# A wait on VectorE for each GpSimd power, with the instruction orders left as they are

## The chip, the cores and the metric

One kernel runs on one core of a Trainium2 chip. The metric is the device time of one execution in microseconds (us). The core's engines run their own instruction streams and meet only at semaphores: TensorE (PE in the profile, with its weight loads as PEld), VectorE (DVE), ScalarE (ACT), GpSimd (POOL) and SyncE (SP), which here only issues transfers.

## What is computed

The reference is one transformer block over 2048 positions and 640 channels, in bfloat16. Cut to what matters:

```
x  = A_q
kv = shift(A_k, 4 taps) * A_v
y  = causal_conv(kv, ssm_k) + kv * ssm_D          # by FFT in the reference
h  = x + layernorm(x) * y
h2 = h + (silu(ln(h) @ w_gate) * (ln(h) @ w_up)) @ w_down
```

There are two layer norms, `layernorm(x)` and `ln(h)`. Each needs, for every position, the mean and one over the square root of the variance plus a small constant.

## The kernel before

**Tiling.** The 2048 positions are cut into four blocks of 512, called j = 0 to 3 in names. A block is 128 partitions by 4 rows (index b); the 640 channels are two halves of 320 (index c). The convolution of block 0 is done with dense transform matrices, that of later blocks with two transform steps on TensorE (`s1`, `s2`), complex products on VectorE (`m1`, `m2` multiply; `ac` adds; `cr`, `ci` combine) and an inverse (`i2`, `i1`). The feed-forward part of a block has, for each slice f of 128 inner channels, two matmul groups (`gu`), a silu on ScalarE (`si`), a copy of the second group out of PSUM by ScalarE into one small buffer (`ue`), and a multiplication on VectorE that reads this buffer (`gm`). There is only one such buffer (pool `UE`), so `ue` of a slice waits for `gm` of the slice before. The `kv` product of blocks 2 and 3 (`kvm`, `kvv`) adds its taps by accumulating transfers that GpSimd issues (`kvd`, line 1089). All matmuls of the main kind show up as line 694, all VectorE tensor-by-tensor operations as line 913, ScalarE's copies out of PSUM as line 677; a name such as `m1003` is product `m1` of block 0, half 0, part 3.

**The norm's statistics.** Each of the two norms ends, for a group of rows, in `ln_rstd` (lines 1009 to 1022), three tiny operations on 128x4 or 128x2 numbers: `va` on VectorE (line 1018, variance plus constant), `nr` on GpSimd (line 1019, power to -0.5) and `nm` on VectorE (line 1021, minus mean times the result). A normalization (`q`, `hn`, lines 1028 and 1029) reads the results of `nr` and of `nm`, on VectorE or ScalarE. `nr` exists 12 times: `nr0j` once per block (the four 128x4), `nr1j` twice per block (the eight 128x2).

**What sets the order.** The program first collects all operations with their dependences, and a planner (`Prog.schedule`) then plays them through with assumed durations and fixes the order on each engine. Priorities and some choices of engine come from a written list (`_ORDER`, `_WHO`). `emit` then writes, for each engine in that order, the semaphore waits that follow from each operation's `deps`, and the operation. A wait stands in front of its operation in the engine's own stream, so what is behind it on that engine is held too.

**The shared port in the planner.** VectorE operations whose names begin with `m1`, `m2`, `ac`, `kv`, `cr`, `ci`, `hn`, `nm`, `q`, `h`, `o` (the last three followed by a digit) or, for blocks 0 and 1, `gm`, carry `o.lock`: the planner takes them to use a port that VectorE shares with GpSimd. It lets no power begin while such an operation runs, and begins no such operation while a power runs (`poolend`). These two rules only shape the planned order. In the program that is written, nothing keeps the two apart.

The planner assumes 0.75 us for a power.

Of the kernel before, what the change touches and what calls it, by code (L numbers as in the profile page):

```python
# [106 lines left out]
class Prog:  # L107
# [147 lines left out]
    def schedule(self, bias):  # L255
        self.dnow, self.rings, self.waiting = 0.0, {"sp": [], "pool": [], "act": []}, []
        self.clock = {"k": -1, "s": 0.5, "busy": {}}
        pemode, dvelock, poolend = 0, False, 0.0
        free = {e: 0.0 for e in self.ENG}
        order = {e: [] for e in self.ENG}  # L260
        ready = []
        for o in self.ops:
            o.ready = o.minready
            if o.npred == 0:
                ready.append(o)
        t = 0.0
        left = len(self.ops)
        while left:
            done_any = True
            while done_any:  # L270
                done_any = False
                for e in ("pe", "dve", "act", "sp", "pool"):
                    if free[e] > t + 1e-9:
                        continue
                    best, held = None, set()
                    waits = e == "dve" and free["pool"] <= t + 1e-9 and any(
                        p.dma is None and p.engs.get("pool", 0) > 0.5 and p.ready <= t - 0.6 for p in ready if "pool" in p.engs)
                    for o in sorted((o for o in ready if e in o.engs and o.force in (None, e) and o.ready <= t + 1e-9), key=lambda o: (o.prio, o.idx)):
                        c = o.engs[e]
                        if e == "pool" and o.dma is None and c > 0.5 and free["dve"] > t + 1e-9 and dvelock:  # L280
                            continue
                        if e == "dve" and o.lock and (poolend > t + 1e-9 or waits):
                            continue
                        if e == "dve" and "act" in o.engs and not o.force:
                            if max(t, free["act"]) + o.engs["act"] <= t + c + bias:
                                continue
                        if e == "act" and "dve" in o.engs and not o.force:
                            if max(t, free["dve"]) + o.engs["dve"] + bias < t + c:
                                continue
                        ok = True  # L290
                        want = {}
                        for tl in o.tiles:
                            if tl.live:
                                continue
                            pl = self.pools[tl.pool]
                            n = want.get(tl.pool, 0)
                            if pl.inorder and (pl.at + n >= len(pl.seq) or pl.seq[pl.at + n] is not tl):
                                ok = False
                                break
                            if tl.pool in held:  # L300
                                ok = False
                                break
                            want[tl.pool] = n + 1
                        if not ok:
                            continue
                        for pn, n in want.items():
                            if sum(1 for f in self.pools[pn].free if f[0] <= t + 1e-9) < n:
                                ok = False
                                if n > 1:
                                    held.add(pn)  # L310
                        if ok:
                            best = o
                            break
                    if best is None:
                        continue
                    o = best
                    done_any = True
                    ready.remove(o)
                    left -= 1
                    for tl in o.tiles:  # L320
                        if not tl.live:
                            pl = self.pools[tl.pool]
                            pl.free.sort(key=lambda f: f[0])
                            _, tl.base, tl.prev = pl.free.pop(0)
                            tl.live = True
                            if pl.inorder:
                                pl.at += 1
                    o.eng, o.start = e, t
                    o.pos = len(order[e])
                    order[e].append(o)  # L330
                    for tl in o.tiles:
                        tl.touch.append(o)
                    if e == "dve":
                        dvelock = o.lock
                    if e == "pool" and o.dma is None and o.engs[e] > 0.5:
                        poolend = t + o.engs[e]
                    if o.dma is None:
                        c = o.engs[e] - self.OVERLAP[e]
                        if e == "pe":
                            c += 0.105 if o.mode != pemode else 0.0  # L340
                            pemode = o.mode
                        free[e] = self.pe_end(t, c, o.slow) if e == "pe" else t + c
                        self.release(o, free[e])
                    else:
                        free[e] = t + o.engs[e]
                        w, pkt, _ = o.dma
                        self.rings[e].append([o, w, pkt, free[e] + self.LEAD])
                    ready += self.waiting
                    self.waiting = []
            nxt = [f for f in free.values() if f > t + 1e-9] + [o.ready for o in ready if o.ready > t + 1e-9]  # L350
            for pl in self.pools.values():
                nxt += [f[0] for f in pl.free if f[0] > t + 1e-9]
            nxt += self.dma_next()
            if not nxt:
                if left:
                    raise RuntimeError("stuck: " + "; ".join(
                        f"{o.name}[{','.join(x.name for x in o.tiles if not x.live)}]" for o in ready[:20]))
                break
            t = max(t, min(nxt))
            self.drain(t)  # L360
            ready += self.waiting
            self.waiting = []
        self.drain(1e6)
        self.order = order
        self.span = max(o.finish for o in self.ops)
# [1024 lines left out]
```

## Time and profile before

| what | value |
|---|---|
| median of four runs | 297.8 us |
| the four runs | 297.42, 298.03, 300.35, 297.56 us |
| the profiled execution: its own time | 297.42 us |
| its span in the profile | 295.6 us |
| so, around the span | 1.8 us |
| TensorE busy | 280.0 us, 95% of the span |
| VectorE busy | 235.5 us, 80% |
| ScalarE busy | 200.5 us, 68% |
| GpSimd busy | 33.2 us, 11% |
| granted TensorE clock | 1.00 of full in every stretch |

Engines are named as above. A row of a timeline has the start in us from the span's beginning, the length in us from the first start to the last end, the engine, the line, the operation with its output and input, how many instructions are merged in the row, and in brackets the idle time before it and who ended it. Rows of VectorE can overlap a little, since one operation starts while the last one drains. A row of waits has who waited for whom, the total in us, how often, and the longest. TensorE's busy time is that of pipelined matmuls with modelled ends, so a busy TensorE is not one at its peak.

### The profile page before, as it was taken

The numbers are of one execution on the slowest core, as the hardware profiler recorded it, in microseconds if no ns is written. First come the engines' busy times: TensorE is split into PE (matmuls) and PEld (weight loads), VectorE is DVE, ScalarE is ACT, GpSimd is POOL, SyncE is SP. The second block draws the span as 40 slices with busy tenths as digits, with TensorE's granted clock in tenths as the row PEclk, the third lists the DMA queues.
The fourth block names the chain that finished last, engine by engine and source line by source line (L and its number), as shares of the span: only waits on it lengthen the run. The fifth ranks groups of instructions, "written<-read, shape, count | busy, mean of one in ns | idle before, by whom it ended". The sixth has DMA issues, their size and how long they took to land.

```text
span 295.6 us, 5187 instructions
## 1 busy us (share of the span) xinstructions
PE 280.0 (95%) x1801; PEld 153.1 (52%) x1820; DVE 235.5 (80%) x479; ACT 200.5 (68%) x484; POOL 33.2 (11%) x31
## 2 busy tenths in 40 slices
PE   7889979799999799999999999999999999999996
PEld 2456645454444366664445467654444676444574
DVE  3999899998999889999999999992899743214422
ACT  3389889999988878778899895768995221242000
POOL 2000500208111130101100304000020020000000
PEclk9999999999999999999999999999999999999999
DMA  6999999834685787727812038754001142000001
GB/s 190 318 354 376 290 365 329 282 116 128 169 179 151 178 205 202 222 73 196 222 41 96 9 83 211 169 137 179 19 0 44 47 90 75 16 0 0 2 22 67
DMA packets 44051, 43.25 MB, mean 146 GB/s; under 512 B 14895, under 2 KB 38889, under 8 KB 43898
## 3 DMA queue, kind: packets, MB, share of 16 engines
q1 hardware_dynamic: 39640, 38.30, 41.6%
q0 software_dynamic: 3328, 3.97, 8.3%
q10 hardware_dynamic: 1058, 0.66, 0.8%
q8 instruction: 14, 0.23, 0.4%
q14 instruction: 11, 0.09, 0.1%
HBM read 20.63 MB, written 2.62 MB: 79 GB/s over the span
## 4 chain that ended last, share of the span: by engine, by line
PE 68%; DVE 12%; ACT 8%; DMA 5%; POOL 3%; issue 2%; SPq 0%; ACTq 0%; DVEq 0%
PE ps L694 67%; DVE sb L913 10%; ACT sb L677 6%; DMA sb<-sb 5%; POOL stt L1019 3%; ACT sb L1029 1%; ACT sb L680 1%; PE ps L823 1%; DVE sb L678 0%; DVE sb L1028 0%; PE ps L1223 0%; DVE sb L681 0%; DVE sb L779 0%; ACT sb L1049 0%; ACT sb L1249 0%
## 5 line engine op out<-in xcount | busy, mean ns | idle before, releaser
L694 PE MATMUL ps<-sb 128*128 128x320 bf16 (+1 forms) x1201 | 224.2, 339 | 8.2 <-DVE sb L913 1.9
L913 DVE TENSOR_TENSOR sb<-sb 128x1280 bf16<-128x1280 bf16 (+3 forms) x286 | 171.0, 656 | 4.0 <-ACT sb L677 3.5
L694 PEld LDWEIGHTS ps<-sb 128*128 128x128 bf16 (+1 forms) x1220 | 116.1, 98 | 100.6 <-issue 8.2
L677 ACT ACTIVATE sb<-ps 128x320 bf16<-128x320 f32 (+2 forms) x282 | 111.5, 483 | 26.0 <-PE ps L694 21.2
L694 PE MATMUL ps<-sb,tab 128*64 128x320 bf16 (+2 forms) x512 | 63.3, 302 | 3.5 <-DMA sb<-sb 2.2
L913 DVE TENSOR_TENSOR sb<-ps,sb 128x512 bf16<-128x512 f32 (+2 forms) x46 | 28.0, 617 | 44.8 <-PE ps L694 38.4
L1249 ACT ACTIVATE sb<-ps 128x512 bf16<-128x512 f32 (+1 forms) x56 | 33.7, 605 | 33.1 <-PE ps L694 32.7
L694 PEld LDWEIGHTS ps<-sb,tab 128*64 128x64 f16 (+2 forms) x512 | 31.6, 101 | 35.6 <-issue 12.8
L1019 POOL TENSOR_TENSOR stt<-stt 128x2 f32<-128x2 f32 (+1 forms) x12 | 19.2, 1603 | 134.2 <-DVE stt L1018 94.4
L1029 ACT ACTIVATE sb<-sb,stt 128x320 bf16<-128x320 bf16 (+1 forms) x31 | 22.3, 749 | 7.0 <-DVE stt L1021 6.6
L680 ACT ACTIVATE sb<-ps 128x320 bf16<-128x320 f32 x49 | 18.5, 447 | 5.1 <-PE ps L694 4.8
L1089 POOL DMA_DIRECT2D sb<-sb x12 | 12.4, 1031 | 68.5 <-DVE sb L913 33.9
L678 DVE CAST sb<-ps 128x320 bf16<-128x320 f32 x26 | 12.0, 479 | 3.4 <-PE ps L694 3.4
L1003 DVE BATCH_NORM_STATS2 stt<-sb 128x6 f32<-128x320 bf16 x32 | 14.4, 474 | 0.0
L1049 ACT ACTIVATE sb<-sb,stt 128x640 bf16<-128x640 bf16 x16 | 13.4, 839 | 0.3 <-DVE stt L1045 0.2
L1042 ACT ACTIVATE sb<-sb 128x640 bf16<-128x640 bf16 x16 | 11.8, 740 | 0.4 <-DMA sb<-in_A_q_dram 0.4
L1028 DVE TENSOR_SCALAR sb<-sb,stt 128x320 bf16<-128x320 bf16 (+1 forms) x17 | 6.2, 383 | 0.7 <-DMA sb<-sb 0.7
L823 PE MATMUL ps<-sb 128*128 128x128 bf16 (+1 forms) x48 | 3.9, 230 | 0.1
L823 PEld LDWEIGHTS ps<-sb 128*128 128x128 bf16 (+1 forms) x48 | 3.2, 119 | 1.5 <-issue 1.1
L1223 PE MATMUL ps<-sb 128*128 128x128 bf16 x40 | 3.1, 219 | 0.9 <-ACT sb L677 0.9
L1021 DVE TENSOR_TENSOR stt<-stt 128x2 f32<-128x2 f32 (+1 forms) x12 | 1.7, 145 | 2.4 <-POOL stt L1019 2.4
L681 DVE TENSOR_SCALAR sb<-ps 128x320 bf16<-128x320 f32 x7 | 3.3, 479 | 0.4 <-PE ps L694 0.4
(24 smaller groups left out, 24.1 us busy)
## 6 DMA issues: line engine op xcount, KB each, us to landing
sb<-sb SPq DMA_DIRECT2D x72, 160.0 KB, 2.2
sb<-sb POOLq DMA_DIRECT2D x12, 320.0 KB, 4.2
out_dram<-sb SPq DMA_DIRECT2D x16, 160.0 KB, 2.0
sb<-in_A_k_dram SPq DMA_DIRECT2D x8, 280.0 KB, 3.7
sb<-in_B_w_down_dram SPq DMA_DIRECT2D x13, 160.0 KB, 7.1
sb<-cst_den SPq DMA_DIRECT2D x8, 256.0 KB, 8.4
sb<-in_A_v_dram SPq DMA_DIRECT2D x6, 320.0 KB, 5.6
sb<-in_A_q_dram SPq DMA_DIRECT2D x6, 320.0 KB, 4.5
```

Of the source, the lines that this page charges most:

```text
L677: fns = {"act": lambda a: a.activation(out=dst(), in_=src(), func=ACTF.Copy), "dve": lambda v: v.tensor_copy(out=dst(), in_=src())}
L678: "dve": lambda v: v.tensor_copy(out=dst(), in_=src())}
L680: fns = {"act": lambda a: a.activation(out=dst(), in_=src(), func=ACTF.Copy, scale=scale), "dve": lambda v: v.tensor_scalar(out=dst(), in0 ...
L694: return lambda t: t.matmul(o(), l(), r(), start=st, stop=sp)
L913: return lambda v: v.tensor_tensor(out=o(), in0=a(), in1=b_(), op=op)
L1003: vec(dve1(CW, False), lambda v: v.bn_stats(st6(l, j, b, c), V(xt, b * D + c * CW, CW)), [(xt, (b, c))], [(ST, ("s", l, j, b, c))], prio, ...
L1019: P.op({"pool": 0.75}, lambda g: g.tensor_tensor(out=y, in0=va, in1=stt[:, 420:420 + hi - lo], op=ALU.pow), c1 + [(ST, "half")], c3, prio, ...
L1029: "act": lambda a: a.activation(out=dst(), in_=src(), func=ACTF.Identity, scale=rs(l, j, b), bias=tmv(l, j, 3)[:, b:b + 1])},
L1042: P.op({"act": act_c(D) + 0.22}, lambda a, b=b, jt=jt: a.activation(out=V(jt, 0, D), in_=V(xt, b * D, D), func=ACTF.Copy, accum_out=tmv(l, ...
L1049: P.op({"act": act_c(D) + 0.3}, lambda a, b=b, jt=jt: a.activation(out=V(jt, 0, D), in_=V(xt, b * D, D), func=ACTF.Square, bias=tmv(l, j, ...
L1089: P.op({"pool": 1.35}, [lambda g: g.dma_start(v4(t0), src(), accum_op=ALU.add)], [(t0, 0)] + cells, [(t0, 0)], prio, dma=(2.1, 2.1, 0.8), ...
L1249: P.op({"act": act_c(n)}, lambda a: a.activation(out=dst(), in_=src(), func=ACTF.Silu), rd, wr, -1000, name=f"si{nm}", after=after)
```

## The change

While the planner fixes the order, it now remembers the last power that it placed on GpSimd (`last`). The next VectorE operation with `o.lock` that it places is given a dependence on that power, and `last` is forgotten.

```
-        pemode, dvelock, poolend = 0, False, 0.0
+        pemode, dvelock, poolend, last = 0, False, 0.0, None
...
                     if e == "dve":
                         dvelock = o.lock
+                        if o.lock and last is not None:
+                            o.deps[last] = 2
+                            last = None
                     if e == "pool" and o.dma is None and o.engs[e] > 0.5:
-                        poolend = t + o.engs[e]
+                        poolend, last = t + o.engs[e], o
```

The dependence is added when the operation has already been placed, so the planner's own play is not touched: the order of the instructions on all five engines is the same in both programs, and only semaphore waits of VectorE differ. For six of the twelve powers the next locked operation is the `nm` that waits for the power already, and nothing differs. For the other six a wait is added:

| power | VectorE operations from `va` to the held one | held operation | operations from it to `nm` |
|---|---|---|---|
| `nr00` | `m2002`, `kvm10` | `m1003` | `m2003`, `ci002`, `kva10` |
| `nr01` | `gm00`, `m1102` | `m2102` | `kvm20`, `ac102`, `ac102`, `cr102` |
| first `nr11` | five small ones, after them the second `va` | `ac200` | none |
| second `nr11` | `ac200`, `nm`, `gm013` | `m1200` | `m2200` |
| `nr02` | `ac212`, `gm16` | `cr212` | `gm17`, `ci212` and nine more |
| first `nr12` | two of the norm's statistics | `h201` | none |

The `nm` of these powers loses its own wait for the power, since the held operation in front of it on the same engine has waited already. (`gm013` reads PSUM and is not locked.)

## The prediction

> **What bounds the kernel now.** I began with the page's busy shares: TensorE 95%, VectorE 80%. TensorE is the bound over most of the span, so a change on VectorE counts only where it makes TensorE late. Then the two rows that the change touches, the power in the list of groups and VectorE's wait for it in the list of waits:
>
> ```profile
> PE 280.0 (95%) x1801; PEld 153.1 (52%) x1820; DVE 235.5 (80%) x479; ACT 200.5 (68%) x484; POOL 33.2 (11%) x31
> ...
> L1019 POOL TENSOR_TENSOR stt<-stt 128x2 f32<-128x2 f32 (+1 forms) x12 | 19.2, 1603 | 134.2 <-DVE stt L1018 94.4
> ```
>
> ```profile
> DVE stt L1021 <- POOL stt L1019: 2.4, 3, 0.9
> ```
>
> Twelve powers take 19.2 us, but VectorE waits for them only 2.4 us in three places. Much of the power's time is therefore something else than work. GpSimd's timeline shows which ones are long:
>
> ```profile
> 30.73 3.72 POOL L1019 TENSOR_TENSOR stt<-stt 128x4 f32<-128x4 f32 x1 [26.34 <-DVE stt L1018]
> ...
> 66.81 5.19 POOL L1019 TENSOR_TENSOR stt<-stt 128x4 f32<-128x4 f32 x1 [11.16 <-DVE stt L1018]
> ...
> 163.27 2.27 POOL L1019 TENSOR_TENSOR stt<-stt 128x4 f32<-128x4 f32 x1 [21.31 <-DVE stt L1018]
> ...
> 183.11 0.71 POOL L1019 TENSOR_TENSOR stt<-stt 128x2 f32<-128x2 f32 x1 [2.54 <-DVE stt L1018]
> ```
>
> And VectorE's timeline beside the first three:
>
> ```profile
> 30.56 2.99 DVE L913 TENSOR_TENSOR sb<-sb 128x640 bf16<-128x640 bf16 x6
> 34.49 0.16 DVE L1021 TENSOR_TENSOR stt<-stt 128x4 f32<-128x4 f32 x1 [0.94 <-POOL stt L1019]
> ...
> 66.64 4.49 DVE L913 TENSOR_TENSOR sb<-sb 128x512 bf16<-128x512 bf16 x7
> 72.04 0.16 DVE L1021 TENSOR_TENSOR stt<-stt 128x4 f32<-128x4 f32 x1 [0.90 <-POOL stt L1019]
> ...
> 163.10 1.55 DVE L913 TENSOR_TENSOR sb<-sb 128x1280 bf16<-128x1280 bf16 x3
> 164.97 5.17 DVE L913 TENSOR_TENSOR sb<-sb 128x512 bf16<-128x512 bf16 x9 [0.32 <-ACT sb L677]
> ```
>
> The reader is to see one thing three times: the power ends when VectorE has paused for 0.9 us, whenever it was issued. VectorE ends its run at 30.56 + 2.99 = 33.55, the power at 34.45, 0.90 later. Then 71.13 and 72.00, 0.87. Then 164.65 and 165.54, 0.89, where the pause was a wait for ScalarE of only 0.32 us; the rest of the power passed beside the next VectorE operation, which took 425 ns where others of its size and line took 415. So the power does not get on while locked VectorE operations follow one another, VectorE's operations are not slowed by it, and a short pause lets it in.
>
> **The change, part by part.** Nothing is moved on any queue, and six waits are added. The price of a wait is the time from the end of the VectorE operation ahead of it to the end of the power (0.89, from the three pairs above) and some 0.04 to wake (34.45 to 34.49), so 0.93 where the power was held off until then. What comes back is the wait of `nm`, if it had one.
>
> *Wait at `m1003` (power `nr00`).* `m2002` and `kvm10` still run ahead, then VectorE pauses 0.93 at about 31.8. `m1003`, `m2003`, `ci002` and `kva10` follow 0.93 later than before, and `nm`, which paused 0.94 before, no longer does: -0.01, and `nm` is where it was. The pause has moved forward over four operations. Behind these wait: `cr003`, `ci003` and `kvv10`, which stand after `nm` in VectorE's own order and so are not later; and TensorE's inverse group for part 2, which needs `ci002`. `ci002` was complete at 32.75 and would be at 33.7; that group's first matmul began at 34.6, after other groups. Hidden by 0.9 us of TensorE's other work; without that cover it would cost up to 0.93. The normalizations on ScalarE wait for `nm` too, so the earlier power (32.7 instead of 34.45) brings them nothing.
>
> *Wait at `m2102` (`nr01`).* The same: 0.93 moved forward from `nm` (0.90) to 67.8, over `m2102`, `kvm20`, two `ac102` and `cr102`; +0.03 from `nm` on. The inverse of this part needs `ci102`, which stands after `nm`. One thing comes earlier: the first `kvd` transfer is queued behind the power on GpSimd and was issued at 71.96. Now it waits for `kvm20` alone, at 70.2. Its reader on VectorE began at 76.6 with the transfer landed at 75.7 already, so an earlier landing saves nothing.
>
> *Wait at `cr212` (`nr02`).* Here nothing comes back: `nm` stands behind eleven more operations and never waited. VectorE reaches the wait at 164.24 and gets on at 164.24 + 0.93 = 165.17 in place of 164.17 (a start can overlap the last one's end): 1.0 later. Of this the old pause for ScalarE, 164.65 to 164.97, absorbs 0.32 and a little overlap: **+0.6 us** on VectorE from `gm17` on. Is there room behind it? All waits of VectorE from 160 to 200 are one row, that same pause:
>
> ```profile
> DVE sb L913 <- ACT sb L677: 0.3, 1, 0.3
> ```
>
> so VectorE carries the 0.6 on. ScalarE's `ue` waits for `gm` (one buffer): it stood idle for VectorE three times from 160 to 180, and its 0.6 is passed on as well. TensorE's own row of matmuls shows no idle time there, but its weight loads show that it waited for ScalarE twice:
>
> ```profile
> 171.25 1.34 PEld L694 LDWEIGHTS ps<-sb 128*128 128x128 bf16 x11 [0.32 <-ACT sb L677]
> ...
> 176.60 0.66 PEld L694 LDWEIGHTS ps<-sb 128*128 128x128 bf16 x6 [0.35 <-ACT sb L677]
> ```
>
> A load that waited for ScalarE gets the 0.6 in full, less what other work in TensorE's order hides, which is little here. After 180 TensorE runs to the end with hardly a gap, so what it loses stays lost. Bounds: 0 (absorbed) to 1.0 (the pause for ScalarE is not there to absorb). I take 0.6.
>
> *The other three.* `ac200` began at 109.98 and its power ended at 109.96: 0.02. `m1200` began at 111.73, power ended 111.35: 0. `h201` began at 183.74, its power ended at 183.82: 0.08 and 0.04 to wake, 0.12 on VectorE; bounds on the end 0 to 0.12, I take 0.05.
>
> *Sum:* 0.0 + 0.0 + 0.6 + 0.05 = +0.65 us. The profiled execution took 297.42 (its span 295.6 and 1.8 around it), so 298.07. The median of the runs shown lies 0.4 above that execution: 298.4.
>
> **A rule of the Trainium skill.** The page "SBUF — State Buffer", section "Who interferes with whom", says that a VectorE instruction with two SBUF inputs contends with a GpSimd instruction that reads SBUF, and that whichever issues first gets the shared pair for the whole instruction while the other fully blocks. The trace agrees that the power is held off, but not how long: at 30.73 it outlasted six VectorE operations, not one. It also disagrees that the other fully blocks: 425 ns beside 415. By the rule VectorE would lose the power's time with or without the wait, and the sum would be 0; by the rows the third power cost VectorE nothing before.
>
> **The rivals.** *The holds are empty or absorbed:* ScalarE's slack takes up the 0.6, or the power enters 0.2 sooner after VectorE's pause than 0.89 (powers beside unlocked operations took 0.70 to 0.72). The time is then the old one, 297.8, give or take 0.3. For it: ScalarE's waits for VectorE between 165 and 180 are two, 0.8 us in all. Against it: they are waits, not slack.
>
> *Clearly slower:* the pauses moved forward are not free. If the four or five operations before each of the first two `nm` feed something that has no cover, each pause costs its 0.93 on TensorE's path, and `cr212` its full 1.0: 2.9 us, 300.7. It decides where TensorE's group for part 2 is reached before 33.7, and likewise by 71.9. A near relative is the `kvd` transfer, which GpSimd now issues while VectorE runs locked operations back to back; held off as the powers were, it would land after 76.6 and hold VectorE up to 1 us. Against that: the issue at 119.96 took 0.88 us in the middle of five such operations.
>
> *Faster:* the powers end 1.8 and 3.3 us sooner, and the `kvd` transfer 1.8. If something waits for them other than through `nm`, up to 1.0 us is won, 296.8. Against it: every reader of a power also waits for `nm`.
>
> **How the numbers follow.** Forecast (0.3 to 1.2 us slower) 0.66; absorbed 0.18; clearly slower 0.10; faster 0.06. About 1%, 3 us, is what a measurement of this kernel can tell from no change. Only the far ends of two cases pass it: faster by over 1% 0.03, slower 0.10, within 0.87. The range goes from 297.1 (half the faster case, on the lower runs) to 299.9 (the forecast with one uncovered pause of 0.93 and the runs' scatter above the median).
>
> **What would show it.** Right: powers `nr00`, `nr01`, `nr02` of 2 us or less ending 0.9 after VectorE's last operation; pauses of 0.9 at line 913 near 31.8, 67.8 and 164.2 that end with the power; no wait of `nm` at 34.5 and 72.0; VectorE at 165 to 180 0.6 late. Wrong: `nm` of block 0 or 1 at another time than 34.5 or 72.0; matmuls late before 160; a `kvd` issue over 1.5 us; `cr212` held for less than 0.7.

## The result, and the profile after

The changed kernel takes 298.28 us in the median of 53 executions (297.21 to 303.79). The kernel before, run beside it, takes 297.74 (79 executions, 296.58 to 303.84). The ratio is 1.0018, with a 95% interval of 1.0007 to 1.0029: slower by 0.5 us, 0.2 to 0.9. The forecast was 298.4. The lower end of the executions moves a little more than the median: the first quartile (a quarter of the executions lie below it) went from 297.24 to 297.98, by 0.74. The ratios here and below leave out executions in a slower state, and they need not be the quotients of the medians beside them: with a dozen executions, a few long ones move a ratio.

The profiled execution of the changed kernel is a long one, 300.14 us with a span of 298.3. So its span cannot be set against the 295.6 of before. 2.0 us of it arise near 140 in a stretch of transfers, which three further profiles of the same kernel pass without that loss (last section), and the reading below goes by stretches.

In the changed file all line numbers are three higher: a power is line 1022, VectorE's tensor-by-tensor operations are line 916, `nm` is line 1024. GpSimd's timeline of the changed kernel, the same four powers as before:

```profile
30.73 1.95 POOL L1022 TENSOR_TENSOR stt<-stt 128x4 f32<-128x4 f32 x1 [26.34 <-DVE stt L1021]
...
67.01 1.85 POOL L1022 TENSOR_TENSOR stt<-stt 128x4 f32<-128x4 f32 x1 [11.36 <-DVE stt L1021]
...
165.23 1.87 POOL L1022 TENSOR_TENSOR stt<-stt 128x4 f32<-128x4 f32 x1 [22.94 <-DVE stt L1021]
...
185.74 0.71 POOL L1022 TENSOR_TENSOR stt<-stt 128x2 f32<-128x2 f32 x1 [2.54 <-DVE stt L1021]
```

The powers that took 3.7, 5.2 and 2.3 us take 1.9. VectorE's timeline beside the first three:

```profile
30.55 1.21 DVE L916 TENSOR_TENSOR sb<-sb 128x640 bf16<-128x640 bf16 x2
32.71 1.86 DVE L916 TENSOR_TENSOR sb<-sb 128x640 bf16<-128x640 bf16 x4 [0.94 <-POOL stt L1022]
34.49 0.15 DVE L1024 TENSOR_TENSOR stt<-stt 128x4 f32<-128x4 f32 x1
...
66.84 1.15 DVE L916 TENSOR_TENSOR sb<-sb 128x512 bf16<-128x512 bf16 x2
68.96 3.43 DVE L916 TENSOR_TENSOR sb<-sb 128x1280 bf16<-128x1280 bf16 x5 [0.97 <-POOL stt L1022]
72.31 0.15 DVE L1024 TENSOR_TENSOR stt<-stt 128x4 f32<-128x4 f32 x1
...
165.05 1.15 DVE L916 TENSOR_TENSOR sb<-sb 128x1280 bf16<-128x1280 bf16 x2
167.20 5.58 DVE L916 TENSOR_TENSOR sb<-sb 128x640 bf16<-128x640 bf16 x10 [1.00 <-POOL stt L1022]
```

The pauses have moved to the waits, and `nm` no longer pauses. `nm00` stands at 34.49 in both kernels; `nm01` is at 72.31 in place of 72.04, and 0.20 of that had arisen before its `va01`. At 165 to 167 there is now a pause of 1.00 where there was one of 0.32 for ScalarE, and no second one behind it. VectorE's list of waits gives the same account:

```profile
DVE sb L916 <- POOL stt L1022: 2.9, 3, 1.0
...
DVE stt L1024 <- POOL stt L1022: 0.6, 1, 0.6
```

Before, `nm` waited 2.4 us in three places. Now VectorE waits 2.9 + 0.6 = 3.5 us for powers. The 0.6 is a wait at 238 that both kernels have.

**A reading that does not depend on where an execution starts late.** Transfers shift whole stretches by some tenths between two profiles of one kernel. The distance between two VectorE operations inside a stretch does not vary so: in three profiles of the kernel before (two of them further down) the distances below agree within 0.015. Each entry is worked out from the start times of the named operations in the trace, in us:

| profile | `va02` to `gm17` | `gm17` to first `nm12` | first `nm12` to the last operation | sum |
|---|---|---|---|---|
| before | 1.94 | 19.16 | 108.64 | 129.75 |
| changed | 2.63 | 19.36 | 108.54 | 130.53 |

The first distance holds the wait at `cr212`, the second the wait at `h201`. From here on the change costs 0.68 to 0.69, then 0.20, and 0.10 of that comes back: 0.78 in all.

What lies ahead of `va02` is not in this sum. `va02` itself stands at 162.78 to 163.27 in the three profiles of the kernel before, and at 162.39 to 162.81 in the three of the changed kernel that have no loss near 140. So no lateness from the early waits shows there. Nor is a gain shown: in two variants without any early wait `va02` stands at 162.47 and 162.88.

### The profile page after: what moved, and what is told of

It is laid out like the page before. It is cut to its first block, busy times and chain, and to the rows that moved or that the text cites. A ratio compares the mean times of both kernels' runs of the same rounds, so it can differ in the third digit from the quotient of the medians.

```text
span 298.3 us, 5190 instructions
## 1 busy us (share of the span) xinstructions
PE 282.2 (95%) x1801; PEld 154.2 (52%) x1820; DVE 235.8 (79%) x479; ACT 200.4 (67%) x484; POOL 27.6 (9%) x31
## 3 DMA queue, kind: packets, MB, share of 16 engines
HBM read 20.63 MB, written 2.62 MB: 78 GB/s over the span
## 4 chain that ended last, share of the span: by engine, by line
PE 61%; DVE 28%; DMA 5%; issue 3%; ACT 1%; SPq 1%; POOL 1%; DVEq 0%; ACTq 0%
PE ps L697 60%; DVE sb L916 23%; DMA sb<-sb 4%; DMA sb<-in_A_q_dram 2%; DVE stt L1006 1%; DVE sb L681 1%; SPq L688 1%; POOL stt L1022 1%; PE ps L826 0%; ACT sb L680 0%; DVE sb L684 0%; ACT sb L683 0%; DVE sb L782 0%; ACT sb L1045 0%; ACT sb L1252 0%
## 5 line engine op out<-in xcount | busy, mean ns | idle before, releaser
L697 PE MATMUL ps<-sb,tab 128*64 128x320 bf16 (+2 forms) x512 | 64.0, 303 | 4.6 <-DMA sb<-sb 3.6
L1022 POOL TENSOR_TENSOR stt<-stt 128x2 f32<-128x2 f32 (+1 forms) x12 | 13.7, 1144 | 137.7 <-DVE stt L1021 96.1
L681 DVE COPY sb<-ps 128x640 bf16<-128x640 bf16 x6 | 2.9, 484 | 0.7 <-PE ps L826 0.5
```

The lines of the kernel that those rows point to most:

```text
L681: "dve": lambda v: v.tensor_copy(out=dst(), in_=src())}
L697: return lambda t: t.matmul(o(), l(), r(), start=st, stop=sp)
L1022: P.op({"pool": 0.75}, lambda g: g.tensor_tensor(out=y, in0=va, in1=stt[:, 420:420 + hi - lo], op=ALU.pow), c1 + [(ST, "half")], c3, prio, ...
```

## The experiments

Two theories at first. Theory A: the wait at `cr212` (power `nr02`) makes nearly all of the cost, and the early waits cost nothing because `nm` gives the pause back. Theory B: the early waits shift transfers, and the lateness near 140 in the profile of the changed kernel is part of its cost.

All ratios below are to the kernel before, run beside the variants. The runs were made in three series (the expectations say "call"). Two controls, which come further down, show how far the ratios can be trusted.

**The changed kernel again** (no edit).

> The changed kernel once more, for a second profile. Its profiled execution took 300.14 us, 1.9 above its median, and TensorE lost 2.0 us of that between 135 and 148, where SyncE's transfers landed late. Theory A (the wait at cr212 is the whole cost, the 2 us belong to that one execution): the time again about 1.002 of the kernel before, and in this profile TensorE's lateness against before steps up by 0.55 us near 167 and by nothing near 140. Theory B (the two early waits shift transfers and so cost something near 140 in the changed kernel generally): a step near 140 here too.

Measured: 298.69 against 297.19, ratio 1.0065 (1.0036 to 1.0093), above what was expected. In the profile, of 297.58 us, there is no lateness near 140: TensorE is 0.6 us earlier there than in the profile of before. The three distances are 2.62, 19.35 and 108.55, as in the first profile. So the step at `cr212` belongs to the kernel and the 2 us near 140 do not belong to every execution. The time is higher than either theory says.

**Without the wait at `cr212`.** The edit:

```
                         if o.lock and last is not None:
-                            o.deps[last] = 2
+                            if last.name != "nr02":
+                                o.deps[last] = 2
                             last = None
```

> The changed kernel without its wait at cr212 (power nr02); the five other added waits stay. Theory A: no pause of 1.0 us at 167, no step there, time as before: ratio 1.000. Theory B (the early waits cost): ratio still about 1.002.

Measured: 297.84 against 297.19, ratio 1.0031 (1.0007 to 1.0055); profiled execution 297.12. VectorE's timeline of this variant at the place:

```profile
162.71 1.54 DVE L917 TENSOR_TENSOR sb<-sb 128x1280 bf16<-128x1280 bf16 x3
164.57 0.83 DVE L917 TENSOR_TENSOR sb<-sb 128x512 bf16<-128x512 bf16 x2 [0.32 <-ACT sb L681]
```

The old 0.32 us pause for ScalarE is back and the long one is gone. `va02` to `gm17` is 1.94, as before; `gm17` to `nm12` is still 19.36, since the wait at `h201` is still there. In the trace theory A is right; in the time the ratio says theory B. A control had to decide.

**The wait at `cr212` alone.** As above with `==` for `!=`.

> The kernel before with the wait at cr212 alone. Theory A: all of the change's cost, +0.55 us, ratio 1.0018, with a pause of VectorE of 0.95 to 1.0 us for the power near 165 and powers nr00 and nr01 as long as before (3.7 and 5.2 us). Theory B: ratio 1.000.

Measured: 298.19 against 297.19, ratio 1.0048 (1.0021 to 1.0074); profiled execution 297.56. Powers `nr00` and `nr02` of this variant:

```profile
30.73 3.72 POOL L1023 TENSOR_TENSOR stt<-stt 128x4 f32<-128x4 f32 x1 [26.34 <-DVE stt L1022]
...
162.71 1.87 POOL L1023 TENSOR_TENSOR stt<-stt 128x4 f32<-128x4 f32 x1 [21.58 <-DVE stt L1022]
```

The first is long again, the third is short. VectorE's row at `cr212` has the long pause:

```profile
164.69 4.11 DVE L917 TENSOR_TENSOR sb<-sb 128x640 bf16<-128x640 bf16 x8 [1.00 <-POOL stt L1023]
```

The distances are 2.62, 19.16 and 108.65: the whole 0.68 with this wait alone, and nothing at `h201`.

**The wait at `cr212`, doubled.** On top of the last variant, GpSimd does this power twice, the first time into a place that nothing reads:

```
-            P.op({"pool": 0.75}, lambda g: g.tensor_tensor(out=y, in0=va, ..., op=ALU.pow), ...)
+            def power(y):
+                return lambda g: g.tensor_tensor(out=y, in0=va, ..., op=ALU.pow)
+
+            extra = [power(tmv(l, j, 1)[:, lo:hi])] * 1 if (l, j) == (0, 2) else []
+            P.op({"pool": 0.75}, extra + [power(y)], ...)
```

> As the run with the wait at cr212 alone, but GpSimd does power nr02 twice, the first time into an unused place, so that the wait is longer by one power, 0.7 to 0.9 us. Theory A: the pause of VectorE is 1.7 to 1.9 us, and since the old 0.32 us pause for ScalarE is used up already, all of the addition arrives at the end: +1.25 to +1.5 us over the kernel before, ratio 1.0042 to 1.0050. Theory C (TensorE has room behind and took only part of the first 1.0): less than half of the addition arrives, +0.9 or less.

Measured: 298.62 against 297.19, ratio 1.0051 (1.0032 to 1.0071); profiled execution 298.97. VectorE's timeline:

```profile
162.95 1.15 DVE L917 TENSOR_TENSOR sb<-sb 128x1280 bf16<-128x1280 bf16 x2
166.09 0.49 DVE L917 TENSOR_TENSOR sb<-sb 128x640 bf16<-128x640 bf16 x1 [1.99 <-POOL stt L1024]
```

The pause grew from 1.00 to 1.99, and `va02` to `gm17` from 2.62 to 3.62; from `va02` to the last operation it is 131.42 against 130.43. All of the added 0.99 arrives at the end, so there is no room behind this place: theory C falls, theory A stands. The second power was longer than expected (0.99 for 0.7 to 0.9), and so was the whole step: 131.42 - 129.75 = 1.67 over the kernel before, for 1.25 to 1.5.

**Two controls and the changed kernel twice more.** The times of the first series were all higher than the traces allow. So the kernel before was run as a variant itself, with no edit, in the two later series, each time beside the changed kernel.

> The kernel before, as a kernel under test: a control. In the first call all four variants came out slower than their traces say (the one whose trace ends 0.3 us sooner than before at 1.0031). Theory S (that offset belongs to the call, not to the variants): this ratio is also about 1.002 to 1.003. Theory V (the variants really have it, outside the one profiled execution): ratio 1.000 within 0.001.

> The changed kernel beside that control. From the steps in the traces (0.68 us at cr212 and 0.10 at h201): 0.8 us above the control, ratio to it about 1.0026. If the change also costs in executions that no profile showed: 1.005 or more above the control.

> The control again, the kernel before as a kernel under test. Theory S (an offset of the call, for whatever is under test): again about 1.003. If the 1.0035 of the first control was chance: 1.000 within 0.001.

> The changed kernel beside the same control: by the steps in the traces, 0.68 and 0.10 us, 0.0026 above the control; steps of 0.68 at cr212 and 0.10 at h201 in this profile too.

| series | kernel before as a variant | changed kernel |
|---|---|---|
| second | 1.0035 (1.0005 to 1.0066) | 1.0045 (1.0019 to 1.0071) |
| third | 1.0004 (0.9979 to 1.0029) | 1.0053 (1.0023 to 1.0083) |

The same program came out at 1.0035 once and at 1.0004 once. With some ten executions of a variant, a ratio here is no better than about 0.3%, and the 1.0031 of the variant without the wait is no evidence for theory B. Theory S (a fixed offset of a series) does not hold either, since the second control is at 1.0004. The changed kernel is 0.0010 and 0.0049 above its controls, where 0.0026 was expected: the scatter is as large as the effect. The traces are sharper. The profile of the first control has the distances 1.94, 19.15 and 108.63, that of the second 1.94, 19.16 and 108.64, exactly those of before, though its `nm01` came at 73.04 instead of 72.04. Those of the changed kernel in these two series have 2.63, 19.35 and 108.54, and 2.63, 19.36 and 108.55.

**`nm` ahead.** The kernel before with no added wait, where `nm00` and `nm01` alone are moved in VectorE's finished order, three places behind their `va`:

```
+        for n in ("nr00", "nr01"):
+            d = order["dve"]
+            i = next(k for k, o in enumerate(d) if o.name == "nm" + n[2:])
+            k = next(k for k, o in enumerate(d) if o.name == "va" + n[2:]) + 3
+            d.insert(k, d.pop(i))
+        for k, o in enumerate(order["dve"]):
+            o.pos = k
         self.order = order
```

> The kernel before, with no added wait, but nm00 and nm01 moved ahead in VectorE's order, to where the changed kernel waits (before m1003 and before m2102). The pause of 0.93 us falls in the same place as in the changed kernel, and nm00 comes at 32.7 in place of 34.5, nm01 at 69.0 in place of 72.0. If normalization was held by the power (theory N): ScalarE's first q begins up to 0.4 us sooner at 34.9, TensorE's 1.3 us wait for ScalarE near 40 shrinks by that, and what remains of it at the end is 0 to -0.4 us. If the norm has cover (theory A): 0.0 at the end.

> nm00 and nm01 ahead, once more beside a control: it was 0.002 below the control, while its trace gave no step on TensorE at 40. Theory A (cover): equal to this call's control within 0.0015. Theory N (a real gain): again 0.002 or more below it.

Measured: 1.0014 (0.9994 to 1.0033) beside the control at 1.0035, then 0.9998 (0.9976 to 1.0021) beside the control at 1.0004. No gain that can be told from none. The trace says why. ScalarE's first two normalizations, in the control and then with `nm` ahead:

```profile
34.87 1.20 ACT L1030 ACTIVATE sb<-sb,stt 128x320 bf16<-128x320 bf16 x2 [0.38 <-DVE stt L1022]
```

```profile
34.45 1.20 ACT L1036 ACTIVATE sb<-sb,stt 128x320 bf16<-128x320 bf16 x2
```

They do begin 0.4 sooner. TensorE's waits from 30 to 60, in the control and with `nm` ahead:

```profile
PE ps L695 <- ACT sb L1030: 1.3, 1, 1.3
PE ps L695 <- DVE sb L914: 1.1, 2, 0.8
```

```profile
PE ps L701 <- DVE sb L920: 2.3, 3, 1.3
```

TensorE's wait of 1.3 us for ScalarE has become one of the same length for VectorE. The norm had cover on both sides.

**The waits right behind `va`.** The kernel before with waits for `nr00`, `nr01` and `nr02` at the first locked operation after `va`:

```
+        for n in ("nr00", "nr01", "nr02"):
+            d = order["dve"]
+            i = next(k for k, o in enumerate(d) if o.name == "va" + n[2:])
+            h = next(o for o in d[i + 1:] if o.lock)
+            h.deps[next(o for o in order["pool"] if o.name == n)] = 2
         self.order = order
```

> The kernel before with the waits for nr00, nr01 and nr02 at the first VectorE operation after va, so that no locked operation runs between. If powers are held off by VectorE's operations alone (theory A): these three take 0.7 to 0.9 us instead of 1.9, VectorE pauses 0.8 to 1.0 us right after va, and the sum is as in the changed kernel, nothing at nm00 and nm01 and 0.6 to 0.7 us at nr02. If a 128x4 power is slow by itself or slow to begin (theory P): they take over 1.2 us, and VectorE's pause is longer by that.

Measured: 300.35 against 297.15, ratio 1.0101 (1.0058 to 1.0143), six executions; the profiled one took 301.25 and is, like the first of the changed kernel, late near 140. The powers of this variant, and VectorE's row behind the third:

```profile
30.73 1.04 POOL L1024 TENSOR_TENSOR stt<-stt 128x4 f32<-128x4 f32 x1 [26.34 <-DVE stt L1023]
...
67.29 1.01 POOL L1024 TENSOR_TENSOR stt<-stt 128x4 f32<-128x4 f32 x1 [11.42 <-DVE stt L1023]
...
165.88 1.03 POOL L1024 TENSOR_TENSOR stt<-stt 128x4 f32<-128x4 f32 x1 [22.92 <-DVE stt L1023]
```

```profile
166.94 1.56 DVE L918 TENSOR_TENSOR sb<-sb 128x1280 bf16<-128x1280 bf16 x3 [1.15 <-POOL stt L1024]
168.83 0.43 DVE L918 TENSOR_TENSOR sb<-sb 128x512 bf16<-128x512 bf16 x1 [0.32 <-ACT sb L682]
```

A power alone takes 1.01 to 1.04, between the two theories' figures but nearer to A: what made it 1.9 to 5.2 is VectorE. The rest of the expectation failed. The pause is 1.15 to 1.19, since VectorE now stands idle from `va` on, while the power is being started; `nm00` is 0.23 late; and at `nr02` the cost is 1.25 (`va02` to `gm17` is 3.19), not 0.6 to 0.7. The second row shows why: the 0.32 us pause for ScalarE is still there. By the program's dependences it is a wait for the copy `ue` of the next slice, which itself waits for `gm16`. With the wait ahead of `gm16` that copy is late by as much as VectorE, and the pause absorbs nothing. In the changed kernel the wait comes behind `gm16`, and ScalarE copies while VectorE stands. This profile ends 3.8 us later than that of before: 0.7 had gathered by 135, 1.9 came between there and `va02`, and 1.25 at `nr02`.

## Why the prediction was right

The forecast was 298.4, measured were 298.28. Step by step:

- *A power ends 0.9 us after VectorE's last operation.* Right in the three places of the changed kernel. VectorE's rows end at 31.76, 67.99 and 166.20, the powers at 32.68, 68.86 and 167.10: 0.92, 0.87, 0.90.
- *Wait at `m1003`: nothing.* Right: `nm00` at 34.49 in both, and in the repeated profile no group of TensorE's is late from 30 to 50. The cover was thinner than the prediction read it, 0.9 us: in the repeated profile `ci002` ends at 33.84, and the group that reads it begins at 34.40, as it does in the first control. 0.56 us were left.
- *Wait at `m2102`: +0.03.* Right in kind: from `va01` to `nm01` 5.47 became 5.54, +0.07, and some operations later, at `gm02`, it is +0.12. What became of it cannot be read off, since transfers shift this stretch by more. For the same reason two of the prediction's signs of being wrong came up and say nothing: `nm01` at another time than 72.0 (72.31; but two profiles of the kernel before have 72.04 and 73.04), and matmuls late before 160 (by 2 us, in one of four profiles of the changed kernel). The `kvd` transfer was issued at 70.82 instead of 71.96 (the prediction had 70.2), in 0.94 us beside locked operations: it is not held off as a power is.
- *Wait at `cr212`: +0.6.* The mechanism is shown by the variants: 0.00 without the wait, 0.68 with it alone, 1.67 with twice the power. The size was off by the wake: VectorE got on 0.10 after the power's end, not 0.04, so the pause was 1.00, not 0.93. At `m2102` it was 0.10 as well, at `m1003` 0.03; why they differ was not found.
- *The step stays to the end.* Right, and the doubled wait is the test: 0.99 of 0.99 arrived. TensorE's weight loads of the changed kernel still wait for ScalarE in the two places:

```profile
173.88 1.34 PEld L697 LDWEIGHTS ps<-sb 128*128 128x128 bf16 x11 [0.53 <-ACT sb L680]
...
179.24 0.66 PEld L697 LDWEIGHTS ps<-sb 128*128 128x128 bf16 x6 [0.35 <-ACT sb L680]
```

- *Waits at `ac200` and `m1200`: 0.02 and 0.* Right: from the first `va11` to these two, 0.01 more and nothing more than before.
- *Wait at `h201`: 0.05.* 0.10 at the end: 0.20 of VectorE, half of which came back behind it.

The terms that the traces show add up to 0.68 + 0.10 = 0.78, where the prediction had 0.65. The direct comparison says 0.54, 0.2 to 0.9, which holds both. The smaller comparisons with ten or so executions lie higher; beside their controls they are 0.001 and 0.005 above. The first quartiles, 0.74 apart, lie close to the 0.78. That the change costs more than 0.78 in some executions is not excluded. That the median came so near the forecast is in part luck: two terms of the sum were larger than forecast, the measured difference of the medians is smaller, and its interval is 0.7 wide.

The rivals: the holds are neither empty nor absorbed (0.68 where nothing was forecast). The early pauses found their cover, so clearly slower did not come. A power that enters sooner than 0.89 did not come either; for it the prediction had compared powers of 128x2 numbers (0.70 to 0.72) with those of 128x4, which take 1.01 to 1.04 alone. Of the earlier powers nothing was won, because every reader waits for `nm` too, and even `nm` ahead won nothing.

The rule of the Trainium skill's page "SBUF — State Buffer" (its section "Summary: rules for kernel authors" states it for two SBUF inputs too), that the later of the two fully blocks until the first has finished, would have made the sum 0 as the prediction read it. The runs show something else in two places. A power was held off through all the locked VectorE operations that followed one another without a pause, 4.5 us of them at 66.6, and not through one only; whose turn it is between two operations the rule leaves open. And the operation that VectorE began with the power still 0.58 us from its end, `gm17`, was not blocked: it took 424 to 426 ns in all six profiles with this overlap. That is not even a slowing: in the variant with the waits behind `va`, with no power running, it took 426 after the same pause. Whether an operation would be blocked that begins just as a power is let in, no run shows: here the power had 0.32 us ahead of it.

## What to carry to other kernels

A wait that keeps two engines apart costs what it makes the waiting engine stand, less what it spares that engine later, and it reaches the end only where nothing behind it has room, as at `cr212`. So look behind each place for the pause it replaces: where the same engine would have waited for the same result a few operations on, the wait only moves; where a short natural pause had let the other engine in, it adds. An engine that takes long in the trace while it is held off costs nothing until someone waits for it. And when effects are a few tenths of a per cent, distances between fixed operations inside a stretch of the trace tell more than a dozen timings, though only of that stretch.

## What the runs showed that was not expected

A 128x4 power on GpSimd takes 1.01 to 1.04 us alone, and 0.87 to 0.92 after VectorE stops if it was issued before; two in a row made VectorE stand 0.99 longer than one.

What lets a power through need not be a pause of VectorE. The fourth 128x4 power, `nr03`, to which the change adds no wait, in the kernel before:

```profile
215.26 1.52 POOL L1019 TENSOR_TENSOR stt<-stt 128x4 f32<-128x4 f32 x1 [28.82 <-DVE stt L1018]
```

And VectorE beside it:

```profile
215.09 0.81 DVE L913 TENSOR_TENSOR sb<-sb 128x1280 bf16<-128x1280 bf16 x1
215.83 1.27 DVE L913 TENSOR_TENSOR sb<-ps,sb 64x512 bf16<-64x512 f32 x2
```

VectorE did not pause, and still the power ended at 216.78, 0.88 after the first of these rows. The two operations behind it take one input from PSUM (`ps`) and carry no `o.lock`. In this case, then, operations with both inputs in SBUF hold a power off, and those two did not.

One stretch of transfers varies. In eleven of the thirteen profiles, both kernels among them, TensorE took as long from 135 to 155 as in the kernel before, or up to 0.8 us less. In two, the first of the changed kernel and the one with the waits behind `va`, TensorE's waits from 135 to 150, shown for the first of these, were:

```profile
PE ps L697 <- DMA sb<-sb: 1.5, 2, 1.3
PE ps L697 <- ACT sb L1252: 0.6, 1, 0.6
```

against this in the kernel before:

```profile
PE ps L694 <- DMA sb<-sb: 0.4, 2, 0.2
```

TensorE lost 2.0 us there in both. In the changed kernel a copy inside SBUF landed 3.6 us after its issue instead of 2.8, and the transfers behind it followed. What tips it was not found; the changed kernel went through without it in its three other profiles. Both profiles are of kernels with early pauses on VectorE (two of eight such profiles, none of the five others), too few to tell whether these make it likelier. The direct comparison speaks against it: 3 of 53 executions of the changed kernel lie 2 us or more above its median, and 10 of 79 of the kernel before.
